# Reordering the first weight loads of a fused attention and feed-forward kernel

## The chip, the core and the metric

The kernel runs on one core of a Trainium2 chip. The metric is the device time of one execution in microseconds; the time before is the median of three runs.

## What is computed

The input x has 2048 rows of 576 bf16 values. It is normalised row by row (xn). Two branches read xn and both are added to x:

```python
xn = _layernorm(x, axis=-1)
return x + _A_ref(xn, A_wqkv, A_wo) + _B_ref(xn, B_w_gate, B_w_up, B_w_down)
```

Branch A is a sliding, dilated attention with 32 heads of 18 columns: `qkv = xn @ wqkv` (576 x 1728), each position attends to itself and the seven positions 2, 4, ... 14 before it, and the result goes through `wo`. Branch B is `(silu(xn @ w_gate) * (xn @ w_up)) @ w_down` with 4608 hidden columns.

## The kernel before

The 2048 positions are held as 128 partitions of 16 rows (R = 16), so "row r" is a tile of 128 positions, one on each partition. Four groups of four rows (NTT = 4) form the outer loop of the second half.

The first half, which the change touches, makes q, k and v. For every row r the normalised tile is turned (576 columns onto partitions, in five slices of 128, the last half empty or doubled), and multiplied by the five slices of `wqkv`: slices 0 to 3 are 128 weight rows each and are held in `wqkv[:, kt, :]`; the last 64 rows are held in `wqkvr` as two halves, output columns 0 to 863 on partitions 0 to 63 and columns 864 to 1727 on partitions 64 to 127. The 1728 output columns are four groups of 432 (G, NG), each in its own PSUM bank. `p_whole(r, t, kt, gs)` multiplies one slice with all 128 partitions for the groups gs. `p_row0_rest` does the last 64 weight rows of row 0 with four matmuls on half the array's rows. `p_row` does a whole later row in such halves.

Row 0 is special: its tile is only centred before the matmuls (`ln_center`), the scale comes in when the banks are emptied (`p_evac`), and TensorE turns it (`transp_pe`). TensorE first runs eleven matmuls on constants (`warm_pe`), then turns row 0, then multiplies row 0 by slices 0, 1 and 2 while row 1 is turned in between, then does slice 0 of row 1, and then slices 3 and 4 of row 0 (lines 486 to 522). ScalarE copies the turned tiles out of PSUM (`copy_pt`): row 0 to `xcT`, row 1 to `xnT`. Later rows are turned by TensorE (`transp_halves`) up to row 4 and by DMA (`transp_dma`) from row 5 on.

The loads go out on two DMA queues, ScalarE's and SyncE's (SP), in the order of the program. Each engine's instructions are in an order written out by hand. All loads, including the x chunks of rows 4 to 15 (line 165) and the first gate and up weights (`load_gu`), sit on SP's queue behind the first weight slices. An issue on SP may wait for an earlier transfer, because eight completion semaphores are used in turn.

The second half loops over four groups of rows and nine chunks of hidden columns: gate and up matmuls (line 611), SiLU and product, then down projection and output projection (line 640). The attention itself runs on VectorE beside these matmuls (`chain`), in pieces that a small queue of costs (`Filler`) places.

Of the kernel before, what the change touches and what calls it, by code (L numbers as in the profile page):

```python
# [17 lines left out]
P = 128  # L18
H, DH, W, DIL = 32, 18, 8, 2
D = H * DH  # L20
HALF = D // 2
G = 432
# [48 lines left out]
def kernel(  # L71
# [11 lines left out]
    nc = tc.nc  # L83
# [45 lines left out]
    wqkv = hTf[:, 0:12 * D].rearrange("p (k j) -> p k j", j=3 * D)  # L129
    wqkvr = hTf[:, 12 * D:12 * D + 2 * G]  # L130
# [13 lines left out]
    def load_x(eng, j):  # L144
        eng.dma_start(xc_b[0][:, j:j + 1, :], x_v[:, j:j + 1, :])

    def load_w(eng, kt):
        if kt < 4:
            eng.dma_start(wqkv[:, kt, :], A_wqkv[kt * P:(kt + 1) * P, :])
        else:  # L150
            for i in range(2):
                eng.dma_start(wqkvr[64 * i:64 * i + 64, :], A_wqkv[4 * P:D, 2 * G * i:2 * G * (i + 1)])

    load_x(nc.scalar, 0)
    load_x(nc.sync, 1)
    load_w(nc.scalar, 1)
    load_w(nc.sync, 0)
    make_identity(nc, ident[:])
    load_w(nc.sync, 2)
    load_x(nc.sync, 2)  # L160
    load_w(nc.sync, 3)
# [34 lines left out]
    def new_ps(name):  # L196
        return ps.tile([P, 512], f32, name=name, tag="ps")
# [35 lines left out]
    def ln_sqrt(r, n=1):  # L233
        c, j = divmod(r, 4)
        xc, xn, mv, rstd = ln[c]
        nc.scalar.activation(rstd[:, j:j + n], mv[:, j:j + n, 1], ACT.Sqrt, bias=eps_t[:], scale=1.0)
# [30 lines left out]
    def transp_pe(r, kts, pt):  # L267
        c, j = divmod(r, 4)
        xn = ln[c][1]
        for i, kt in enumerate(kts):  # L270
            nc.tensor.transpose(pt[:, i * P:(i + 1) * P], xn[:, j, kt * P:(kt + 1) * P], ident[:])  # L271
# [4 lines left out]
    def copy_pt(eng, r, kts, pt):  # L276
        eng(xT_of(r)[:, kts[0]:kts[-1] + 1, :],
            pt[:, 0:len(kts) * P].rearrange("p (k t) -> p k t", t=P))
# [29 lines left out]
    def p_mm(t, g, kt, half, r, start, stop):  # L308
        rows = slice(0, P) if half is None else slice(64 * half, 64 * half + 64)
        return nc.tensor.matmul(t[g][:, 0:G], xT_of(r)[rows, kt, :], w_at(g, kt, rows),  # L310
                                start=start, stop=stop)

    def p_whole(r, t, kt, gs=range(NG)):
        for g in gs:
            p_mm(t, g, kt, None, r, kt == 0, False)
# [14 lines left out]
    def p_row(r, between=None, at=(0, 1), t=None):  # L330


        done = t is not None
        t = t or [None] * NG
        fence = {}
        for swap in range(2):
            for i in range(2):
                for kt in (0, 1, 2, 3) if swap else (0, 4, 1, 2, 3):
                    if done and kt == 0:
                        continue  # L340
                    for half in range(2):
                        g = i + 2 * (half ^ swap)
                        if t[g] is None:
                            t[g] = new_ps("qkv_ps")
                        mm = p_mm(t, g, kt, half, r, swap == 0 and kt == 0, swap == 1 and kt == 3)
                        if swap == 0 and kt == 3 and half == 1:
                            fence[i] = fence_after(mm)
                        if swap and kt == (1 if done else 0) and half == 0:
                            fence_before(mm, fence[i])
                    if swap and (i, kt) == at and between is not None:  # L350
                        between()
        return t
# [130 lines left out]
    def turn(r):  # L483
        return lambda: transp_halves(r)
# [20 lines left out]
    t = [new_ps("qkv_ps") for g in range(NG)]  # L505
    p_whole(0, t, 0)
    p_whole(0, t, 1)
    p_whole(0, t, 2, (0,))
    transp_pe(1, (0, 1), pt1)
    transp_pe(1, (2,), pb)  # L510
    copy_pt(nc.scalar.copy, 1, (0, 1), pt1)
    p_whole(0, t, 2, (1, 2))
    transp_pe(1, (3, 4), pb[:, P:])
    copy_pt(nc.scalar.copy, 1, (2, 3, 4), pb)
    p_whole(0, t, 2, (3,))
    ln_sqrt(0)
    u = [None] * NG
    for g in (0, 2, 1, 3):
# [26 lines left out]
    t = p_row(2, turn(3))  # L545
# [6 lines left out]
    t = p_row(3, turn(4))  # L552
# [10 lines left out]
    for r in range(4, R):  # L563
        t = p_row(r)
# [92 lines left out]
    for tt in range(NTT):  # L657
# [28 lines left out]
        for sub in range(0, RT, 2):  # L686
            t, fence = {}, {}
# [36 lines left out]
```

## Time and profile before

| what | us |
|---|---|
| median of three runs | 503.4 (503.15 to 503.45) |
| the profiled execution | 503.37 |
| its span, first to last instruction | 501.6 |
| TensorE busy | 497.6 |
| VectorE busy | 329.3 |
| ScalarE busy | 200.9 |

The times in the profile are counted from the first instruction. Its page gives the busy share of each engine, the chain of work that ended last, groups of instructions by line, and the DMA issues with the time from issue to landing. PE is TensorE's matmul row, PEld its weight loads, DVE is VectorE, ACT is ScalarE, SPq and ACTq are the issues on the queues of SyncE and ScalarE. In a timeline line the first number is the start, the second the length, and a note in brackets says how long the engine was idle before it and what released it. Several instructions of one kind that follow each other are merged into one line with a count. By these lines the qkv matmuls of the first half run from 5.87 us to 59.72 us, and the rest of the span is the second half.

### The profile page before, as it was taken

To read this page: it belongs to the slowest core of one execution; us is meant where nothing else is said; L and a number is where in the kernel's file an instruction comes from. 1 tells how busy PE (TensorE), PEld (TensorE's weight loads), DVE (VectorE), ACT (ScalarE), POOL (GpSimd) and SP (SyncE) were. 2 spreads that over 40 slices of the span, in tenths; PEclk is the share of its full clock that TensorE was granted. 3 is DMA by queue.
4 is the path that set the end of the run, shared out by engine and by line. 5 is a ranking of instruction groups with operands and counts; after the bars stand their busy time and mean duration, and the time that the engine had idled before them with its cause. 6 is when DMAs were issued, how large, how long until landed. Compare 5 with 4: busy or idle time off the path is not lost.

```text
span 501.6 us, 13271 instructions
## 1 busy us (share of the span) xinstructions
PE 497.6 (99%) x5795; PEld 283.1 (56%) x5795; DVE 329.3 (66%) x479; ACT 200.9 (40%) x416; POOL 2.7 (1%) x9
## 2 busy tenths in 40 slices
PE   9999999999999999999999999999999999999997
PEld 4555544444677644444777544445777444446775
DVE  5888597898999698999897139995980222221001
ACT  4756657645300255554300445557000454553000
POOL 1000000000000000000000000000000000000000
PEclk9999999999999999999999999999999999999999
DMA  8799989898731045535640154453700335432200
GB/s 311 175 205 238 306 271 293 259 322 260 194 117 61 25 143 189 190 110 177 158 132 29 31 182 153 132 189 110 183 25 14 101 115 177 158 127 39 76 14 25
DMA packets 77186, 75.42 MB, mean 150 GB/s; under 512 B 22708, under 2 KB 72528, under 8 KB 77128
## 3 DMA queue, kind: packets, MB, share of 16 engines
q1 hardware_dynamic: 76840, 73.98, 49.7%
q8 instruction: 45, 0.74, 0.6%
q10 hardware_dynamic: 288, 0.59, 0.3%
q14 instruction: 13, 0.11, 0.1%
HBM read 58.76 MB, written 5.90 MB: 129 GB/s over the span
## 4 chain that ended last, share of the span: by engine, by line
PE 99%; DVE 0%; issue 0%
PE g_ps L611 56%; PE d_ps L640 32%; PE qkv_ps L310 11%; PE warm_ps L174 1%; PE pt L271 0%; DVE ot L654 0%; PE pt L292 0%; PE warm_ps L271 0%; PE warm_ps L177 0%
## 5 line engine op out<-in xcount | busy, mean ns | idle before, releaser
L611 PE MATMUL g_ps<-xnT,gu 64*128 64x512 bf16 x2592 | 280.4, 376 | 0.0
L611 PEld LDWEIGHTS <-gu 64*128 64x128 bf16 x2592 | 126.1, 94 | 152.9
L622 ACT ACTIVATE sg<-g_ps 128x512 bf16<-128x512 f32 x144 | 87.3, 606 | 156.6 <-PE g_ps L611 156.6
L640 PE MATMUL d_ps<-wd,hT 64*128 64x288 bf16 x2304 | 146.3, 283 | 0.0
L640 PEld LDWEIGHTS <-hT 64*128 64x128 bf16 x2304 | 112.0, 94 | 29.8
L624 DVE TENSOR_TENSOR hT<-sg,uc 128x512 bf16<-128x512 bf16 x144 | 60.2, 419 | 93.9 <-ACT uc L623 93.8
L623 ACT CAST uc<-g_ps 128x512 bf16<-128x512 f32 x144 | 85.2, 592 | 0.0
L423 DVE TENSOR_REDUCE PP<-PP 128x64 f32<-128x1152 bf16 x64 | 84.9, 1347 | 0.4
L310 PE MATMUL qkv_ps<-hT,xnT 64*128 64x432 bf16 (+1 forms) x536 | 50.0, 342 | 0.0
L418 DVE TENSOR_TENSOR PP<-QO,Kr 128x2304 bf16<-128x2304 bf16 (+1 forms) x35 | 43.5, 1251 | 7.3 <-DMA Kr<-hT 6.9
L652 DVE TENSOR_TENSOR ot<-d_ps,xr 128x288 bf16<-128x288 f32 x30 | 12.3, 451 | 51.0 <-PE d_ps L640 51.0
L450 DVE TENSOR_TENSOR PP<-Vr,A 128x2304 bf16<-128x2304 bf16 (+1 forms) x35 | 43.3, 1251 | 0.4
L310 PEld LDWEIGHTS <-xnT 64*128 64x128 bf16 (+1 forms) x536 | 26.1, 94 | 22.3 <-ACT xnT L296 0.2
L455 DVE TENSOR_TENSOR PP<-PP 128x2304 bf16<-128x2304 bf16 x24 | 32.5, 1354 | 0.3
L622 ACT ACT_TABLE_LOAD x5 | 6.4, 1283 | 47.2 <-PE g_ps L611 47.2
L640 PE MATMUL d_ps<-wo,xnT 64*128 64x288 bf16 x288 | 22.9, 283 | 0.0
L372 ACT CAST hT<-qkv_ps 128x288 bf16<-128x288 f32 (+2 forms) x58 | 20.9, 423 | 0.0
L443 ACT ACTIVATE PP<-PP 128x1024 f32<-128x1024 f32 x4 | 4.2, 1056 | 31.3 <-DVE PP L439 31.2
L640 PEld LDWEIGHTS <-xnT 64*128 64x128 bf16 x288 | 14.0, 94 | 3.6
L654 ACT CAST ot<-d_ps 128x288 bf16<-128x288 f32 x1 | 0.4, 399 | 38.8 <-PE d_ps L640 38.8
L372 ACT CAST QO<-qkv_ps 128x432 bf16<-128x432 f32 (+1 forms) x30 | 12.2, 406 | 8.3 <-PE qkv_ps L310 8.2
L221 DVE BATCH_NORM_STATS2 stats<-wd 128x6 f32<-128x288 bf16 x32 | 12.8, 440 | 0.0
(56 smaller groups left out, 92.1 us busy)
## 6 DMA issues: line engine op xcount, KB each, us to landing
gu<-in_B_w_gate_dram SPq DMA_DIRECT2D x36, 512.0 KB, 3.8
gu<-in_B_w_up_dram SPq DMA_DIRECT2D x36, 512.0 KB, 5.2
wd<-in_B_w_down_dram SPq DMA_DIRECT2D x9, 576.0 KB, 6.2
kv_d<-hT SPq DMA_DIRECT2D x5, 576.0 KB, 6.1
gu<-in_B_w_gate_dram SPq DMA_DIRECT2D x36, 64.0 KB, 4.9
gu<-in_B_w_up_dram SPq DMA_DIRECT2D x36, 64.0 KB, 4.5
xr<-in_A_x_dram SPq DMA_DIRECT2D x8, 288.0 KB, 3.9
out_dram<-ot SPq DMA_DIRECT2D x16, 144.0 KB, 1.8
```

Source lines behind the costliest of these rows:

```text
L221: nc.vector.bn_stats(sums[r][:, k, :], xc[:, j, k * HALF:(k + 1) * HALF])
L310: return nc.tensor.matmul(t[g][:, 0:G], xT_of(r)[rows, kt, :], w_at(g, kt, rows), start=start, stop=stop)
L372: (nc.vector.tensor_copy if n in dve else nc.scalar.copy)(*parts[n])
L418: nc.vector.tensor_tensor(prod[:, a:b], QO[:, RT * tt + a:RT * tt + b, :], Kr[:, s:s + b - a, :], op=ALU.mult)
L423: nc.vector.tensor_reduce(L[:, w, rs], prod[:, rs].rearrange("p r (h d) -> p r h d", d=DH), axis=AX.X, op=ALU.add)
L450: nc.vector.tensor_tensor(dst[:, a:b], Vr[:, s:s + b - a, :].rearrange("p r (d h) -> p r d h", h=H), A[:, w, a:b].unsqueeze(2).to_broadcas ...
L455: nc.vector.tensor_tensor(dst, acc, pv, op=ALU.add)
L611: mm = nc.tensor.matmul(ring_ps[j][b][:], gu[rows, slot, k, fc], xnT[rows, kt, tok], start=(swap == 0 and kt == 0), stop=(swap == 1 and kt ...
L622: nc.scalar.activation(sg[:], t[0][:], ACT.Silu)
L623: nc.scalar.copy(uc[:], t[1][:])
L624: nc.vector.tensor_tensor(hT[:, ch * FC + j, :], sg[:], uc[:], op=ALU.mult)
L640: mm = nc.tensor.matmul(t[sub][h][:, 0:HALF], a[rows], w[rows, h * HALF:(h + 1) * HALF], start=(swap == 0 and n == 0), stop=(swap == 1 and ...
```

## The change

Three loads and one place in TensorE's order are altered.

- Weight slice 0 now goes out on ScalarE's queue behind row 0 of x, where slice 1 was. Slice 1 goes out on SP's queue behind row 1 of x, where slice 0 was, as two transfers of 864 columns each.
- The last 64 weight rows are loaded with one transfer where there were two. Its destination is the whole of `wqkvr` with 128 partitions; its source is the 64 x 1728 block, read as two column halves of 64 rows one after the other.
- TensorE multiplies row 0 by slice 2 for two column groups, where it was one, before it turns the first part of row 1; the other two groups stand between the two parts of that turn.

```diff
         if kt < 4:
             eng.dma_start(wqkv[:, kt, :], A_wqkv[kt * P:(kt + 1) * P, :])
         else:
-            for i in range(2):
-                eng.dma_start(wqkvr[64 * i:64 * i + 64, :], A_wqkv[4 * P:D, 2 * G * i:2 * G * (i + 1)])
+            eng.dma_start(wqkvr, A_wqkv[4 * P:D, :].rearrange("r (i c) -> i r c", i=2))
 
     load_x(nc.scalar, 0)
     load_x(nc.sync, 1)
-    load_w(nc.scalar, 1)
-    load_w(nc.sync, 0)
+    load_w(nc.scalar, 0)
+    for i in range(2):
+        nc.sync.dma_start(wqkv[:, 1, 2 * G * i:2 * G * (i + 1)], A_wqkv[P:2 * P, 2 * G * i:2 * G * (i + 1)])
     make_identity(nc, ident[:])
     load_w(nc.sync, 2)
     load_x(nc.sync, 2)
...
     p_whole(0, t, 0)
     p_whole(0, t, 1)
-    p_whole(0, t, 2, (0,))
+    p_whole(0, t, 2, (0, 1))
     transp_pe(1, (0, 1), pt1)
     transp_pe(1, (2,), pb)
     copy_pt(nc.scalar.copy, 1, (0, 1), pt1)
-    p_whole(0, t, 2, (1, 2))
+    p_whole(0, t, 2, (2, 3))
     transp_pe(1, (3, 4), pb[:, P:])
     copy_pt(nc.scalar.copy, 1, (2, 3, 4), pb)
-    p_whole(0, t, 2, (3,))
     ln_sqrt(0)
```

## The prediction

> **What bounds the kernel now.** I read the share of busy time and the chain that ended last first, then that chain in order of time, then the start-up instruction by instruction, then the DMA issues, and last the stretches with their clock.
>
> The page gives TensorE 99% of the span, and the chain runs almost wholly through it:
>
> ```profile
> span 501.6 us, 13271 instructions
> PE 497.6 (99%) x5795; PEld 283.1 (56%) x5795; DVE 329.3 (66%) x479; ACT 200.9 (40%) x416; POOL 2.7 (1%) x9
> PE 99%; DVE 0%; issue 0%
> ```
>
> The chain in order of time (start, length, what) shows how little waiting the start holds:
>
> ```profile
> 5.20 0.11 PE warm_ps L177
> 5.31 0.53 PE pt L271 x5
> 5.84 0.03 issue
> 5.87 2.11 PE qkv_ps L310 x9
> 7.98 0.11 PE warm_ps L271 x2
> ```
>
> So a microsecond lost at the start is lost at the end, and there is hardly one to win. The timeline of the first 27 us has the places that the change touches:
>
> ```profile
> 3.07 1.34 SPq L152 DMA_DIRECT2D hT<-in_A_wqkv_dram  x2
> 5.45 0.27 ACT L277 COPY PP<-pt 128x128 bf16<-128x128 bf16 x1 [0.96 <-PE pt L271]
> 5.76 0.21 PEld L310 LDWEIGHTS <-PP 128*128 128x128 bf16 x2 [0.20 <-ACT PP L277]
> ...
> 8.13 0.37 ACT L277 COPY xnT<-warm_ps 128x256 bf16<-128x256 bf16 x1 [1.47 <-PE warm_ps L271]
> 8.55 0.56 PEld L310 LDWEIGHTS <-xnT 128*128 128x128 bf16 x4
> 8.64 0.89 PE L310 MATMUL qkv_ps<-hT,xnT 128*128 128x432 bf16 x4
> ...
> 9.37 1.36 PE L310 MATMUL qkv_ps<-hT,PP 128*128 128x432 bf16 x8
> 10.20 0.11 PEld L310 LDWEIGHTS <-PP 64*128 64x128 bf16 x4 [0.36 <-issue]
> ```
>
> Read here: the last 64 weight rows (slice 4) go out from 3.07 as two transfers, and TensorE first needs them at 10.20. Their landing, by the rows of their source line (issue to landing, min/median/max):
>
> ```profile
> L152 SPq DMA_DIRECT2D hT<-in_A_wqkv_dram x2: 465/513/561, 3.1 to 3.9; - x2
> DMA to landing us min/median/max: 5.9/6.2/6.5
> ```
>
> The second went out at 3.95 and landed 5.9 later, at 9.89: 0.3 us to spare. The stretches give the rate of all sixteen DMA engines and, at the very end, the clock (last columns: granted clock, DMA share, GB/s):
>
> ```profile
> 3.10:6.50 3.40, 3.37 (x13) 1.45 (x12) 2.34 (x8) 1.48 (x6) 0.66 (x1) 1.00 1.03 410
> 500.00:501.45 1.45, 0.00 (x0) 0.00 (x0) 0.00 (x0) 0.00 (x0) 0.00 (x0) 1.00 0.18 64
> 501.46:501.60 0.14, 0.00 (x0) 0.00 (x0) 0.00 (x0) 0.00 (x0) 0.00 (x0) 0.50 0.00 0
> ```
>
> The sum is made against the profiled execution, 503.37 us with a span of 501.6 and 1.8 around it; the median of the runs is 503.4, so the two agree to 0.03.
>
> **Slice 0 and slice 1 change places.** The queues carry the same bytes as before: row 0 of x and one slice on ScalarE's. Issue times hardly move: slice 0 goes out at 1.17 instead of 1.19. Before, slice 0 landed at 5.83 and slice 1, behind row 0, at about 6.3. The first matmul began at 5.87, when the weight load of 5.76 (0.1 us), released by ScalarE's copy (5.45 + 0.27 = 5.72), was through. So an earlier slice 0 gains nothing here; one as late as slice 1 was would cost 0.5 us, of which TensorE at half rate loses half (its 128x512 warm-up matmuls took 4.42/10 = 0.44 us each, and the 128x432 ones after 6.5 us take 0.18). Since the other queue now holds rows half as long, slice 0 should get more than half of the engines' turns and land by about 5.6: I take 0, ends -0.1 and +0.3.
>
> **Slice 1 in column halves** makes 256 rows of 1,728 B out of 128 of 3,456 B. In the trace's packet records (no view prints them) these take 72 and 135 ns, so an engine pays 16 x 72 - 8 x 135 = 72 ns more, and slices 2 and 3 land 0.07 later. Slice 3 landed at 2.59 + 6.5 = 9.14 and is wanted at 9.37, so this is covered. SP issues one transfer more here (0.43) and one fewer at slice 4 (0.5); both SP orders then stand at the wait for row 0 of x (3.93) and go on together from 3.95. The x chunks, the gate and up loads and the ring fills behind them wait on completions that are renumbered by one transfer; what they feed is priced below.
>
> **Row 1 turned one matmul later.** From the second of the first two transposes, 0.22 us to its end, the copy (8.13 + 0.37), the release and weight load (8.55 to 8.65) take 0.78 us to the first row-1 matmul. Before, 0.77 us of TensorE work lay between, so the chain fitted exactly. Now one matmul of 0.18 stands ahead instead of between: TensorE waits 0.18 us at 8.64. Only if slice 4 comes late is that hidden, because the wait ends at slice 4 anyway.
>
> **Slice 4 as one transfer** is the large item. The source is now walked as two blocks of 64 rows of 864 columns: the outermost count of its pattern is 2, where all other weight slices have 128. The trace's completion records bear on this: a 128-row load completes in sixteen steps, the fill of a ring row as 1 x 14 x 576 in fourteen and one early step for the rest, the 15-row halo in fifteen and one early. The spread follows the outer count, and none of before's transfers has one under 14. With 2, two engines carry 216 KB, 110.6 kB each, and the other fourteen nothing.
>
> The Trainium skill, "DMA: Bandwidth & Descriptors", section on why a DMA increments its semaphore by 16, says that the number of engines is the largest up to 16 that divides the slowest dimension of both patterns; that gives 2 here, and the completion records agree with it. The same page's rule table advises one 128-partition transfer in place of two on partition halves; by that alone slice 4 would land a few tenths of a microsecond earlier and the time would be about 503.5, the first rival below.
>
> Price of two engines: at 410/16 = 25.6 GB/s each, 110.6 kB take 4.3 us. By the packet records the 64 rows of one engine cost 64 x 72 ns = 4.6 where least disturbed and 64 x 101 = 6.5 at the median of slice 4 in before, when sixteen engines wrote the same 64 partitions at once. I take 4.6, since two engines alone don't crowd, with 4.3 and 6.5 as ends. The transfer starts when these two engines are through with slice 3, whose shares landed between 8.13 and 9.14; from 8.6 it lands at 8.6 + 4.6 = 13.2 (12.4 to 15.6). TensorE then starts the four matmuls of slice 4 at 13.3 instead of 10.20: **+3.1 us** (+2.3 to +5.5).
>
> What is late next: row 3 of x lies behind slice 4 on those two engines and lands near 13.7 instead of 10.2. VectorE takes it behind row 0's evacuation, which itself waits for slice 4, at about 14.6. The chunks of rows 4 to 7 come near 16 and are wanted at 14.46 + 3.1 = 17.6; the first gate and up weights come near 24 and are wanted at 59.7 + 3.1. SP stands at the small up load until slice 4 has landed, then at row 3, and the transposes behind it (19.10 before, held by VectorE) move by VectorE's 3 us. I cost all that at nothing. The sum: 503.4 + 3.1 + 0 (the 0.18 is inside the wait) = **506.5 us**.
>
> **The rivals.**
> (a) The merged transfer is dealt to sixteen engines anyhow. Then only the 0.18 at row 1 is left, less up to 0.1 for slice 0: 503.5, not slower by anything that can be told. For it speaks that the destination still has 128 rows; against it the fourteen and fifteen steps above. It decides from the point where slice 4 lands by 10.3.
> (b) The pause slows TensorE's clock. At the end of the trace the clock stood at 0.50 from 501.46 on, 2.97 us after the last matmul had ended (498.49); here TensorE idles from about 10.3 to 13.3, 3.0 us. At the start it took from 0.77 to about 6.5 us of work to reach full rate, so the loss is between 0 and half of 5.7, about 1.6 in the middle: 508.1. For it speaks the nearness of 3.0 to 2.97; against it, that the pause may end before the clock falls.
> The Trainium skill, "TensorE: Matmul & The Clock Gate", part 1, tells of a free-running window of 3.4 us in which an idle TensorE falls to half its clock; by its window the loss would be 3.4/2 = 1.7 us, and whether 3.0 us of idleness meet it depends on the window's phase. The 0.50 above agrees.
> (c) Slice 0 lands as late as slice 1 did and nothing else changes: 503.4 + 0.25 + 0.18 = 503.8. The packet turns speak against it.
>
> **How the numbers follow.** Two engines without a slower clock 0.45, with it 0.33, rival (a) with (c) 0.12, all else (one engine, crowding as in before, a second late load) 0.10. The likeliest gives 506.5. The range takes in the first two with the ends of their price: 505.4 (503.4 + 2.3 less some tenths for noise) to 508.8 (508.1 with a slow start of slice 4). A measurement of this kernel can tell about 0.2%, 1.0 us, from no change. Faster by more would need more than the whole of TensorE's waiting and half-rate work before 6.5 us, 0.2 + 0.3 us: 0.02. Within it: 0.11. Slower: 0.87.
>
> **What would show it.** In the profile after: the merged transfer lands 8.5 us or more after its issue at about 3.95; a wait of TensorE of about 3 us for the weights at the four half-row matmuls that were at 10.20; row 3's statistics after 14 us; no new wait after 20 us; and, for (b), matmul spacings of 0.36 instead of 0.18 just behind the wait. I am wrong if that transfer lands by 10.3, or if a later wait gives time back.

## The result

The changed kernel takes 509.81 us (median of four runs, 509.51 to 510.39), the kernel before 503.35 (503.15 to 503.45): a ratio of 1.013, 95% interval 1.0113 to 1.0148. It is slower by 6.5 us. The forecast of slower held, but 509.81 lies above the range of 505.4 to 508.8, and the rise is twice the predicted 3.1.

The profiled execution of the changed kernel took 509.58 us. Its page:

```profile
span 507.8 us, 13271 instructions
PE 498.8 (98%) x5795; PEld 312.1 (61%) x5795; DVE 329.4 (65%) x479; ACT 201.1 (40%) x416; POOL 2.7 (1%) x9
```

The chain in order of time now begins with DMA waits, and holds none after 15 us:

```profile
0.73 3.18 DMA wd<-in_A_x_dram
3.91 0.02 issue
3.93 11.01 DMA hT<-in_A_wqkv_dram
14.94 0.04 issue
14.98 3.63 PE qkv_ps L310 x22
18.61 0.14 PE pt L292 x10
18.75 3.10 PE qkv_ps L310 x34
```

The merged transfer goes out at 3.93 and lands 11.01 us later. The timeline shows what waits for it:

```profile
5.59 1.62 PE L310 MATMUL qkv_ps<-hT,PP 128*128 128x432 bf16 x8
7.60 0.53 PE L310 MATMUL qkv_ps<-hT,PP 128*128 128x432 bf16 x2 [0.39 <-DMA hT<-in_A_wqkv_dram]
...
9.52 0.89 PE L310 MATMUL qkv_ps<-hT,PP 128*128 128x432 bf16 x4
14.98 0.90 PE L310 MATMUL qkv_ps<-hT,PP 64*128 64x432 bf16 x4 [4.57 <-DMA hT<-in_A_wqkv_dram]
15.65 2.95 PE L310 MATMUL qkv_ps<-hT,xnT 64*128 64x432 bf16 x18
```

The four half-row matmuls start at 14.98 instead of 10.20, after 4.57 us without work. The eighteen behind them take 2.95 us, where eighteen of the same form took 1.80 before, so TensorE runs at half rate for most of them. The line of before:

```profile
10.57 1.80 PE L310 MATMUL qkv_ps<-hT,xnT 64*128 64x432 bf16 x18
```

The stretches of the changed kernel give the clock (the last three columns are granted clock, DMA share and GB/s):

```profile
10.40:14.50 4.10, 0.01 (x1) 0.03 (x1) 0.14 (x1) 0.00 (x0) 0.00 (x0) 1.00 1.02 291
14.54:14.95 0.41, 0.00 (x0) 0.00 (x0) 0.00 (x0) 0.00 (x0) 0.00 (x0) 0.50 0.99 325
15.00:17.90 2.90, 2.90 (x18) 1.39 (x19) 1.67 (x4) 1.78 (x4) 0.00 (x0) 0.50 1.02 321
17.96:21.00 3.04, 3.04 (x46) 1.80 (x43) 2.12 (x8) 2.00 (x6) 0.58 (x1) 1.00 0.24 62
```

By the trace's clock record the half rate stands from 14.54 to 17.95. Of it 17.95 - 14.98 = 2.97 us fall on work, which costs 1.49. The sum is 14.98 - 10.20 = 4.78 for the later start and 1.49 for the clock, 6.27 us; the spans differ by 507.8 - 501.6 = 6.2.

### The profile page after: what moved, and what is told of

The parts are those of the page before. It is cut to its first block, busy times and chain, and to the rows that moved or that the text cites. A ratio compares the mean times of both kernels' runs of the same rounds, so it can differ in the third digit from the quotient of the medians.

```text
span 507.8 us, 13271 instructions
## 1 busy us (share of the span) xinstructions
PE 498.8 (98%) x5795; PEld 312.1 (61%) x5795; DVE 329.4 (65%) x479; ACT 201.1 (40%) x416; POOL 2.7 (1%) x9
## 4 chain that ended last, share of the span: by engine, by line
PE 96%; DMA 3%; DVE 0%; issue 0%
PE g_ps L610 55%; PE d_ps L639 31%; PE qkv_ps L310 10%; DMA hT<-in_A_wqkv_dram 2%; DMA wd<-in_A_x_dram 1%; DVE ot L653 0%; PE pt L292 0%
## 5 line engine op out<-in xcount | busy, mean ns | idle before, releaser
L610 PEld LDWEIGHTS <-gu 64*128 64x128 bf16 x2592 | 139.1, 94 | 140.0
L639 PEld LDWEIGHTS <-hT 64*128 64x128 bf16 x2304 | 123.7, 94 | 18.2
L310 PE MATMUL qkv_ps<-hT,xnT 64*128 64x432 bf16 (+1 forms) x536 | 51.3, 348 | 0.0
L310 PEld LDWEIGHTS <-xnT 64*128 64x128 bf16 (+1 forms) x536 | 29.1, 96 | 20.7 <-issue 1.5
L639 PEld LDWEIGHTS <-xnT 64*128 64x128 bf16 x288 | 15.5, 94 | 2.2
```

What stands on the lines that cost most here:

```text
L610: mm = nc.tensor.matmul(ring_ps[j][b][:], gu[rows, slot, k, fc], xnT[rows, kt, tok], start=(swap == 0 and kt == 0), stop=(swap == 1 and kt ...
L639: mm = nc.tensor.matmul(t[sub][h][:, 0:HALF], a[rows], w[rows, h * HALF:(h + 1) * HALF], start=(swap == 0 and n == 0), stop=(swap == 1 and ...
```

## The experiments

**The merged transfer undone, the rest kept.**

```diff
-            eng.dma_start(wqkvr, A_wqkv[4 * P:D, :].rearrange("r (i c) -> i r c", i=2))
+            for i in range(2):
+                eng.dma_start(wqkvr[64 * i:64 * i + 64, :], A_wqkv[4 * P:D, 2 * G * i:2 * G * (i + 1)])
```

> The changed kernel with the last 64 weight rows again as two transfers; all else of the change stays. Theory (the merged transfer alone costs the time, since two DMA engines carry it): it lands by 10.0 us, TensorE waits for nothing at the half-row matmuls, 503.2 to 503.8 us. Rival (slice swap, halves and later turn carry part of the loss): clearly above, from 505 to 509.

Measured: 503.57 us against 503.33 (ratio 1.0004, 0.9995 to 1.0013). The slice swap, the halves and the later turn together cost nothing that these rounds can tell. Slice 4 landed at 10.57, later than the expected 10.0, but the half-row matmuls, which start at 10.74 here, stand no further behind the matmul ahead of them than in the kernel before. The profile has one new wait, for slice 2, and then no other before the half-row matmuls:

```profile
7.75 0.52 PE L311 MATMUL qkv_ps<-hT,PP 128*128 128x432 bf16 x2 [0.56 <-DMA hT<-in_A_wqkv_dram]
```

**The merged transfer alone, in the kernel before** (the same lines the other way round).

> The kernel before with the merged transfer alone. Theory: the whole loss is here, 509 to 510.5 us, with a TensorE wait of 4.5 us for the weights and a stretch of 3.4 us at half clock. Rival (the loss needs the new order of the slices): 503.4 to 506.

Measured: 509.90 us (ratio 1.0133, 1.0119 to 1.0147), the whole loss. Its waits of TensorE in the first 40 us (total, times, longest):

```profile
PE qkv_ps L309 <- DMA hT<-in_A_wqkv_dram: 5.6, 2, 5.4
```

The longer wait is 5.4 us, where 4.5 was expected, because TensorE came to it earlier there; the transfer landed at 15.13. The half clock stands from 14.45 to 17.87, as in the changed kernel.

**One transfer still, but walked in 128 rows.** Only the source's pattern changes. In this kernel and the two with four and eight blocks, the weight rows lie on other partitions than the multiplication needs, so the last slice is multiplied wrongly; the work is the same.

```diff
-            eng.dma_start(wqkvr, A_wqkv[4 * P:D, :].rearrange("r (i c) -> i r c", i=2))
+            eng.dma_start(wqkvr, A_wqkv[4 * P:D, :].rearrange("r (i c) -> (r i) c", i=2))
```

> The changed kernel with the merged transfer's source walked as 128 rows of 864 columns, one after the other, instead of two blocks of 64: one transfer still, same bytes, same packets of 1,728 B, only the outermost count differs (the weight rows lie on other partitions than the multiplication needs, so the last slice is multiplied wrongly). Theory (the outermost count sets how many engines carry it): lands by 9.9 us, 503.2 to 503.8 us. Rival (one transfer of 216 KB is slow there however it is walked): 509 to 510.5.

Measured: 503.52 us (ratio 1.0004, 0.9995 to 1.0013). The transfer landed at 9.47. So it is not the merging that is slow, but the outermost count of 2. The 128 packets are of the same size, and on sixteen engines at once they took 71 to 82 ns.

**Four and eight blocks.**

```diff
-            eng.dma_start(wqkvr, A_wqkv[4 * P:D, :].rearrange("r (i c) -> i r c", i=2))
+            eng.dma_start(wqkvr, A_wqkv[4 * P:D, :].rearrange("r (i c) -> (r i) c", i=2).rearrange("(b a) c -> a b c", a=4))
```

> The changed kernel with the merged transfer's source walked as four interleaved blocks of 32 rows of 864 columns (weight rows on other partitions than the multiplication needs, so the last slice is multiplied wrongly). Theory (as many engines as the outermost count, a fixed time per packet): four engines with 32 packets each, at 72 to 108 ns 2.3 to 3.5 us instead of 6.2, landing at 10.9 to 12.3 us, a wait of 0.6 to 2 us, too short to halve the clock: 504.0 to 505.5 us. Rival (any pattern in blocks is as slow as two blocks): 509 to 510.5.

> The same with eight blocks of 16 rows. Theory: eight engines with 16 packets each, 1.2 to 1.7 us, landing at 9.8 to 10.5 us, a wait of 0 to 0.3 us: 503.3 to 504.0 us. Rival: 509 to 510.5.

Measured: 507.72 us with four blocks (ratio 1.0092, 1.0077 to 1.0107) and 504.37 with eight (1.0026, 1.0017 to 1.0035). The landings, 12.84 and 11.09, and the waits of 2.42 and 0.59 fall with the count, against the rival, but both landings and both times missed their range. The half-row matmuls, first with four blocks, then with eight:

```profile
12.88 0.54 PE L310 MATMUL qkv_ps<-hT,PP 64*128 64x432 bf16 x4 [2.42 <-DMA hT<-in_A_wqkv_dram]
```

```profile
11.14 0.54 PE L310 MATMUL qkv_ps<-hT,PP 64*128 64x432 bf16 x4 [0.59 <-DMA hT<-in_A_wqkv_dram]
```

With four blocks the clock fell even so; the mean granted clock (1 is full speed) was 0.996 to 0.997 in all four executions. Three lines of the profiled one's stretches:

```profile
10.05:13.45 3.40, 0.98 (x11) 0.45 (x10) 0.50 (x2) 0.20 (x1) 0.00 (x0) 1.00 1.03 311
13.50:16.80 3.30, 3.30 (x30) 1.77 (x28) 1.64 (x4) 1.49 (x5) 0.54 (x1) 0.50 1.05 368
16.90:20.00 3.10, 3.10 (x46) 1.96 (x44) 2.90 (x11) 1.89 (x6) 0.00 (x0) 1.00 0.49 130
```

TensorE had been at work again from 12.88, 0.6 us before the clock fell at 13.46; it was busy for 0.98 of the 3.4 us before that. The full 3.41 us at half clock fell on work and cost 1.7 us, with 12.88 - 10.20 = 2.7 for the start 4.4; the spans differ by 505.9 - 501.6 = 4.3. With eight blocks the packets were most of the miss: from 8.5 us on they took 116 to 139 ns by the medians of half a microsecond each, not 72 to 108.

**Matmuls on constants in the pause.**

```diff
     p_whole(0, t, 3)
+    for i in range(75):
+        nc.tensor.matmul(u[3][:, G:512], nc.const_aps.tensor(1.0, [P, P], bf16), nc.const_aps.tensor(1.0, [P, 512 - G], bf16),
+                         start=False, stop=False)
     p_row0_rest(t)
```

> The changed kernel with 75 small matmuls on constants (128x80 each, into unused columns) ahead of the four half-row matmuls, so that TensorE works through its wait. Theory (the wait makes the clock fall to half for 3.4 us, which costs 1.5 us of the 6.4): the wait for the weights stays until about 15 us, the clock stays full, 508.0 to 508.5 us. Rival (the clock costs nothing, all is wait): 509.5 to 510.5.

Measured: 509.20 us (508.50 to 510.54; ratio 1.0119, 1.0105 to 1.0134), above what was expected. The profiled execution, 508.50, shows the mechanism:

```profile
10.14 3.08 PE L522 MATMUL qkv_ps<-const-bfloat16-1.0 128*128 128x80 bf16 x75
14.95 0.54 PE L310 MATMUL qkv_ps<-hT,PP 64*128 64x432 bf16 x4 [1.73 <-DMA hT<-in_A_wqkv_dram]
15.31 1.82 PE L310 MATMUL qkv_ps<-hT,xnT 64*128 64x432 bf16 x18
```

The weights come at the same time, 14.95, but the eighteen matmuls behind take 1.82 us, full rate, and the feed-forward matmuls begin at 64.48 instead of 65.95: 1.47 us won, what the half clock was reckoned to cost. Of it 0.36 goes back in this execution: its chain stands at "DMA xnT<-QO", the turned attention output, at 134.4, and the 648 down-projection matmuls take 40.05 us instead of 39.69. The three other executions took up to 2.0 us more and were not profiled. The slowest, 510.54, had a mean granted clock of 0.997, as one stretch of 3.41 us at half clock makes of such a span, so it seems to have lost the clock once, where isn't known; the other two had 1.000, and what slowed them stays open. By the times alone this kernel can't be told from the changed one; the 1.47 us rest on the profile.

**The later loads held back.** A store of 64 loaded weights ahead of the x chunks makes SP wait until the merged transfer has landed.

```diff
     load_x(nc.sync, 3)
+    hold = dram.tile([1, 64], bf16, name="hold")
+    nc.sync.dma_start(hold[:], wqkvr[0:1, 0:64])
     for c in range(1, 4):
```

> The changed kernel with one 128-byte store of loaded weight rows put on SP's queue ahead of the x chunks of rows 4 to 15, so that these and all later loads go out only when the merged transfer has landed. Theory (its packets took about 108 ns instead of 72 because the other fourteen engines moved x chunks beside it): packets of about 72 ns, landing near 13.2 us, first half-row matmul near 13.3 us, 506.3 us with the clock kept and up to 508 with the clock halved. Rival (two engines pay about 100 ns a packet by themselves): landing near 14.9 us, 509.3 to 510.5.

Measured: 508.25 us (507.60 to 508.38; ratio 1.0105, 1.0088 to 1.0122); the profiled execution was the 507.60. In it the matmuls start at 13.39, and the packets took 72 to 82 ns throughout: the loads that ran beside them had slowed them. The time still missed the expected 506.3, and one reason is that the held loads come late elsewhere, a wait of 0.71 for a row turned by DMA:

```profile
13.39 0.54 PE L312 MATMUL qkv_ps<-hT,PP 64*128 64x432 bf16 x4 [3.08 <-DMA hT<-in_A_wqkv_dram]
27.49 2.73 PE L312 MATMUL qkv_ps<-hT,xnT 64*128 64x432 bf16 x28 [0.71 <-DMA xnT<-wd]
```

13.39 - 10.20 = 3.19 and 0.71 make 3.9 of the 4.2 us by which its span of 505.8 is longer. In this execution the clock stayed full in spite of a pause of 3.08 us (mean granted clock 1.000), although the shorter pause of four blocks halved it. The other three, 508.24 to 508.38, had 0.996 to 0.997, so they lost about one stretch of 3.41 us to the half clock; they were not profiled, and where it fell isn't known. So the same kernel can keep the clock or lose it. Two neighbouring stretches of the profiled execution, cut where the clock record puts their ends:

```profile
8.75:12.10 3.35, 1.56 (x8) 0.68 (x7) 1.11 (x5) 0.81 (x3) 0.00 (x0) 1.00 0.13 51
12.15:15.50 3.35, 2.11 (x30) 1.34 (x31) 1.52 (x4) 1.70 (x4) 0.00 (x0) 1.00 0.28 50
```

The pause is cut in two, and TensorE was busy for 1.56 and 2.11 of 3.35 us in the two stretches.

**The later turn alone**, and **the slices alone** (the rest of the kernel before unchanged):

```diff
-    p_whole(0, t, 2, (0,))
+    p_whole(0, t, 2, (0, 1))
...
-    p_whole(0, t, 2, (1, 2))
+    p_whole(0, t, 2, (2, 3))
...
-    p_whole(0, t, 2, (3,))
```

> The kernel before with the later turn of row 1 alone. Prediction: a wait of TensorE of 0.18 us at the first row-1 matmul, 503.5 us. Rival (the weight load overlaps, or other work fills it): a wait under 0.1 us; the time can't tell the two apart, the profile can.

```diff
-    load_w(nc.scalar, 1)
-    load_w(nc.sync, 0)
+    load_w(nc.scalar, 0)
+    for i in range(2):
+        nc.sync.dma_start(wqkv[:, 1, 2 * G * i:2 * G * (i + 1)], A_wqkv[P:2 * P, 2 * G * i:2 * G * (i + 1)])
```

> The kernel before with slice 0 and slice 1 in each other's places (slice 1 in halves) alone. Theory (slice 0 lands earlier, near 5.2 to 5.5 us, but the weight load behind ScalarE's copy ends hardly before 5.9 where the clock is still halved, and slices 2 and 3 land no earlier): 503.0 to 503.5 us, inside the noise. Rival (the halves make the later slices late enough to lose more than the earlier start wins): 504 us or more.

Measured: 503.26 us against 503.08 for the turn (ratio 1.0003, 0.9994 to 1.0012), 503.87 against 503.27 for the slices (1.0010, 1.0001 to 1.0019), above the expected 503.0 to 503.5. The turn leaves 0.10 us between the last transpose's 0.05 and the first row-1 matmul (matmul starts 8.21 and 8.36), not 0.18: the matmul starts with its weight load, not behind it. The slices alone are at most slightly slower: slice 2 landed at 7.47 instead of 7.22, slice 3 at 9.52 instead of 9.14.

## Why the prediction was right and wrong

**Right.** The mechanism of the wait is shown. Two shares carried the merged transfer: the completion records of its semaphore show one early step at 5.04 and then 14.80 and 14.94; with four blocks there are four steps after the early one (11.91 to 12.84), with eight there are eight (10.29 to 11.09). The loss is in that transfer alone, follows the outermost count and vanishes when the same bytes are walked in 128 rows. The Trainium skill's rule on the number of engines ("DMA: Bandwidth & Descriptors", section on why a DMA increments its semaphore by 16) agrees with these counts; the advice in the page's rule table to use one 128-partition transfer held only where the source was walked in 128 rows. TensorE's wait stands where it was put, no later wait followed, and nothing was recovered.

**The step that failed: the packet price.** The result lies 3.3 us above the likeliest 506.5. Of this 1.7 are the transfer (4.78 instead of 3.1) and 1.5 the slower clock, which the likeliest case put at nothing. For the transfer I took 64 x 72 ns = 4.6 us, "since two engines alone don't crowd". The packets ran from 7.91 to 14.09, 6.2 us or 97 ns each: 72 for the first fourteen of an engine and then about 108. That is near the upper end, 101 ns, which I had from slice 4 of before and set aside. With the loads held back they took 72 to 82, so the step failed because the other fourteen engines were not idle. The rate of all engines shows that it was mutual; first the changed kernel, then the kernel before:

```profile
9.00:14.00 5.00, 1.41 (x8) 0.57 (x6) 0.97 (x5) 0.66 (x3) 0.00 (x0) 1.00 1.02 298
```

```profile
10.00:13.50 3.50, 3.50 (x48) 1.84 (x48) 2.94 (x10) 2.64 (x7) 0.58 (x1) 1.00 1.02 413
```

By the packet records the 4,608-byte packets of the x chunks went from 182 to 252 ns (medians) while the merged transfer ran. From my 13.2 to the measured 14.94 this is 1.6 of the 1.7 us. The rest is small by luck: the packets began 0.7 us before my 8.6, and the landing came 0.85 us after the last packet had ended, for which my sum had no term.

**The rival that came true beside the likeliest.** I gave the slower clock 0.33 and priced it at 1.6; it cost 1.49. That the size is near is luck: 1.6 was the middle of 0 to 2.85, and the trace has one stretch of 3.41 us at half clock, of which 2.97 fell on work. The nearness of 3.0 to 2.97 was no threshold either: at the end of the changed kernel's trace the clock fell 4.77 us after the last matmul (504.70 and 509.47). With a wait of 4.6 us the clock fell in all four executions of the changed kernel: their mean granted clock is 0.992 to 0.997, where the profiled execution before had 1.000. That the longer wait was needed for it is not shown: with 3.08 us, about the pause that I had forecast, three executions of four show the slower clock, and with 2.42 us all four do. So this was a second step that failed: the case without the slower clock was not the likelier one.

**The range.** I let it end at 508.8, where the slower clock met the likeliest price of the transfer and a slow start. The upper end of the transfer with the clock's middle price, 503.4 + 5.5 + 1.6 = 510.5, would have held the result. Two costs of one cause can come together, and the range had to take their sum.

**Small terms.** Slice 0 landed at 5.55 (I had 5.6). I priced the halves of slice 1 at 0.07 later for the next slices; slice 2 landed at 7.56, 0.34 later, and since the full clock came at 4.30 us in this execution instead of 6.53, TensorE reached it early and waited 0.39. This and the turn's 0.10 are hidden by the wait for slice 4, as was said of the turn.

## What to carry to other kernels

The outermost count of a DMA's access pattern decided here on how many engines it ran: before two transfers are merged, look which dimension the merged pattern walks slowest, and put a long one there, as the 128 rows were. Price a transfer on few engines at the rate it has beside the traffic that will really run, not at its rate when undisturbed. A pause of TensorE costs its own length and can cost a stretch at half clock besides; whether it does hangs on how the pause falls, so its price belongs in the range.

## What was not expected of the hardware

- A transfer on two engines slowed the other fourteen: all sixteen together moved 298 GB/s instead of 413, for 5 us. Packets of 1,728 B took 72 to 82 ns on two engines with nearly nothing beside them (51 GB/s in all), and 71 to 82 on sixteen engines that walked 128 rows (410 GB/s). With the x chunks beside them they took about 108 on two engines and 114 to 125 on four. So a high rate alone does not slow them. Where the engines meet is not settled: no run here separates the memory that they write from the memory that they read.
- In these records the clock changes only at instants that lie whole multiples of 3.41 us apart, whatever the work is doing then: the full clock came at 4.30 and fell at 14.54, 10.24 = 3 x 3.41 later, and came back 3.41 after that; with four blocks the distances are 6.83 and 3.41. "TensorE: Matmul & The Clock Gate" of the Trainium skill, part 1, has this free-running window, and the records agree. They add a bound: the clock fell after a pause that filled a whole stretch and after a stretch in which TensorE was busy for 0.98 of 3.4 us, and stayed after one with 1.56 of 3.35. If it is the busy share that decides, the least share that keeps the clock lies somewhere between 29% and 47%; these are two executions, and no run varies the share alone. A pause of 2.4 us lost the clock where one of 3.1 kept it.
